# A decode step's last weight matrix: 128 of its rows moved to sixteen partitions by a transfer of their own

## The chip, the core and the metric

The kernel runs on one core of a Trainium2 chip. The metric is the device time of one execution in microseconds (us). TensorE (PE in the profile, its weight loads PEld) multiplies matrices, VectorE (DVE), ScalarE (ACT) and GpSimd (POOL) work on vectors, and SyncE (SP) issues nearly all transfers between the chip's memory (HBM) and the on-chip memory (SBUF). A core has 16 DMA engines; a transfer is shared out over several of them, and is done when the last of these is done. Matmul results go to the accumulators (PSUM).

## The reference

One decode step for a batch of B = 4 rows of width D = 576. Two branches read the same normalised input and are added to it:

```python
xn  = layernorm(x)
# A: attention over a window of 2048 keys, 16 kv heads of 128, 2 query heads each
q   = xn @ wq
p   = softmax(q . k_cache[:, :, -2048:] * 128**-0.5)
a   = (p . v_cache[:, :, -2048:]) @ wo
# B: a token mixer and an MLP, F = 4608
h   = gelu(layernorm(xn) @ w1)
x1  = xn + shifted(h) @ w2            # sequence length 1
b   = x1 + gelu(layernorm(x1) @ w3) @ w4
out = x + a + b
```

Nearly all the work is reading: the keys and the values are 33.5 MB each, wq and wo 4.7 MB each, w3 and w4 5.3 MB each. All of it is bf16.

## The kernel before

The kernel is one list of operations for each engine. `add` and `add_dma` put an operation on an engine's list with the signals that it waits for and a number, `key`; each list is then sorted by `key`, and an engine runs its list in that order. An operation with several waits starts after the last of them, and everything behind it on its engine waits too.

**Loads.** SP issues in this order: wq, w2, w1, w3, then the key blocks (one per kv head, 2 MB each, all 128 partitions, 16 KB a partition) into a ring of four slots (`kring`), the value blocks into another ring of four (`vring`), wo into the key ring after the keys, and last w4 into the value ring. A block's load waits until the block four before it has been used (`T...` for keys, `PV...` for values). Every one of these loads is issued at line 176, inside `add_dma`.

**w4.** `w4_src` (line 245) gives each partition p the RT = 36 consecutive rows 36p to 36p + 35 of w4, so that column t of the tile holds the rows 36p + t. The loads come in five pieces of rows per partition, `W4P = ((0, 14), (14, 28), (28, 33), (33, 35), (35, 36))`.

**Stages of TensorE.** The projections of q and of the mixer come first. Then `pe_h2` (line 527) multiplies the normalised x1 with w3 in five steps r (four of 128 rows, one for the rest), each into four groups of 32 columns of the array (j = 0..3, 1152 outputs each) and three accumulators (`CH2`). `gelu2` (line 537, three activations) applies gelu, and a transpose by VectorE (line 540) makes of it `h2T_sb`, the left operands of the w4 product. `zeroS` (line 340) waits for `gelu2` and opens the key stage: transposes of key blocks (line 351), their copies to SBUF (lines 358 and 359) and the scores (line 367). `SC15` is the last score product. After the softmax the value stage follows, a hardware loop over the 16 blocks (`PV`, line 448), each scaled by VectorE (line 456).

**The end.** After the value loop TensorE runs, in this order: `turn` (line 474), which waits for the last scaling; `AO` (line 463, 64 matmuls), the product with wo, which waits for `ORT`, the copy of `turn`'s result by VectorE (line 477); `MO0` (line 463, 28 matmuls), rows 0 to 13 of each partition of w4; `fold` (line 543, 8 matmuls with an ACT copy at line 553 before it), which adds up four partial accumulators; `MO1` to `MO4` (line 543, 88 matmuls), the other pieces of w4, each waiting for its piece. `AO` and `MO0` use four column groups of the array in turn (`acc_mm`, 288 columns wide), `MO1` to `MO4` two (`fin_mm`, 144 wide). Two copies to `out_sb` (lines 570 and 571) and two stores end the kernel.

```python
def acc_mm(e, h, lhsT, rhs, start=False, stop=False, k0=0):
    return e.matmul(ACC[h], lhsT=lhsT, rhs=rhs, start=start, stop=stop, tile_position=(k0, 32 * h))
...
add("pe", pe_turn, waits=[("c", ("on", m), NIT + 1) for m in range(4)] + ["sel32"], sig="turn", key=KV + 19.9)
...
add("pe", pe_AO, waits=["ORT", ev_wo], sig="AO", key=KV + 20)
```

Of the kernel before, what the change touches and what calls it, by code (L numbers as in the profile page):

```python
# [6 lines left out]
BF16 = mybir.dt.bfloat16  # L7
ACTF = mybir.ActivationFunctionType
# [11 lines left out]
WO_AFTER = 3  # L20
V0_AFTER = 8
FOLD = 14
W4P = ((0, 14), (14, 28), (28, 33), (33, 35), (35, 36))


class Op:
# [12 lines left out]
def bass_parallel_sum__sliding_block_cached__mixer_s_mlp__decode_kernel(  # L39
    nc, A_x, A_k_cache, A_v_cache, A_wq, A_wo, B_x, B_w1, B_w2, B_w3, B_w4, out  # L40
):
    B, Sq, D = A_x.shape
    _, Hkv, Sk, Dh = A_k_cache.shape
    Hq = A_wq.shape[1] // Dh
    F = B_w3.shape[1]
    W = min(4096, max(256, Sk // 4))
    assert (B, D, Hkv, Dh, Hq, W, Hq // Hkv, F) == (4, 576, 16, 128, 32, 2048, 2, 4608)
    G = Hkv
# [4 lines left out]
    EPS = 1e-5  # L53
    HALF = D // 2
    FH = F // 2
    RT = F // 128
    N2 = F // 4
    CH2 = [(0, 12), (12, 24), (24, 32)]
    x2 = A_x.rearrange("b s d -> (b s) d")
    o2 = out.rearrange("b s d -> (b s) d")  # L60
# [1 line left out]
    with ExitStack() as ctx:  # L62
        def sb(name, shape, dt):
            return ctx.enter_context(nc.sbuf_tensor(name, shape, dt))
# [7 lines left out]
        regB_t = sb("regB", [128, max(NKT * 1024, W3E)], BF16)  # L72
# [4 lines left out]
        w3main = regB_t[:, 0:4 * F].rearrange("p (r n) -> p r n", r=4)  # L77
        w3rag = regB_t[:, 4 * F:W3E]
# [23 lines left out]
        x1nT = sb("x1nT", [128, 6, 32], BF16)  # L102
        hs_inT = sb("hs_inT", [128, 10, B], BF16)
        h2T_sb = sb("h2T_sb", [128, RT, 32], BF16)
        Qpad_t = sb("Qpad", [128, 130 * G], BF16)
        Qpad = Qpad_t[:, 0:128 * G].rearrange("p (g b c) -> p g b c", g=G, b=B)
        Qs = sb("Qs", [128, 4, B, 32], BF16)
# [14 lines left out]
        PTb = sb("PTb", [128, NT * 32], BF16)  # L122
# [13 lines left out]
        ps = ctx.enter_context(nc.psum_tensor("ps", [128, 8, 512], FP32))[:]  # L136
# [13 lines left out]
        H2ps = [ps[:, k, 0:RT * (z - a)] for k, (a, z) in enumerate(CH2)]  # L150
        h_sb = PTs[0:B].rearrange("p t r -> p (t r)")[:, 0:D]
        xsrc = PTs[0:B].rearrange("p t r -> p (t r)")[:, 640:1920].rearrange("b (s p) -> b s p", s=10)
        h2a = PTb[:, 0:N2].rearrange("p (c i) -> p c i", i=32)

        S = {}
        for nm in ("pe", "dve", "act", "pool"):
# [8 lines left out]
        def add(engine, emit, waits=(), sig=None, key=0.0, loop=None):  # L165
            seqc[0] += 1
            prog[engine].append(Op(emit, waits, sig, key, seqc[0], loop))

        def add_dma(pairs, skey, waits=(), key=0.0, engine="sp"):
            if skey not in S:  # L170
                S[skey] = sem("s_" + "_".join(str(k) for k in (skey if isinstance(skey, tuple) else (skey,))))
            dma_count[skey] = dma_count.get(skey, 0) + 16 * len(pairs)

            def emit(e):
                for o_, i_ in pairs:
                    e.dma_start(o_, i_).then_inc(S[skey], 16)  # L176
            add(engine, emit, waits, None, key)
            return ("dma", skey, dma_count[skey])
# [4 lines left out]
        KS = float(NHB + 4)  # L183
        KV = KS + 4.0
# [3 lines left out]
        P = lambda *a, **k: add("pool", *a, **k)  # L188
# [3 lines left out]
                                    pattern=[[-1, 128]], channel_multiplier=1), waits=["ib1"], sig="ident_bf", key=-98)  # L192
        P(lambda e: e.memset(ragsrc[:], 0.0), sig="rag_zero", key=-97)
        P(lambda e: e.memset(xsrc, 0.0), sig="xs_zero", key=-96.8)
        P(lambda e: e.memset(xnT[:], 0.0), sig="xnT_zero", key=-96.6)
        P(lambda e: e.memset(Qpad_t[:], 0.0), sig="qpad_zero", key=-96)
        P(lambda e: e.memset(x1nT[:], 0.0), sig="x1nT_zero", key=-95.9)
# [2 lines left out]
        def first_counts(e):  # L200
# [37 lines left out]
        for g in range(G):  # L238
            kk = KS + g if g else V0_AFTER + 0.5
            w = [f"PV{g - NVS}"] if g >= NVS else (["hT"] if g < WQ_SLOTS else [])  # L240
            ev_v.append(add_dma(kv_pairs(vring_t, g % NVS, A_v_cache, g), ("v", g % NVS), w, kk))
            if g == WO_AFTER:
                ev_wo = add_dma([(kring_t[:, 0:32 * D], A_wo.rearrange("(p r) n -> p (r n)", r=32))],
                                "wo", [wo_wait], kk + 0.1)
        w4_src = B_w4.rearrange("(p r) n -> p r n", r=RT)
        w4_sb = vring_t[:, 0:RT * D].rearrange("p (t n) -> p t n", n=D)
        for n, (t0, t1_) in enumerate(W4P):
            lst = (t1_ * D - 1) // UE
# [124 lines left out]
        for n in range(NHB):  # L373
            p = n % 32
            w = [("L", ("k", p // 8), 16)] if p % 8 == 0 else []
            w.append(("L", ("eb", (p - NTB) % 32), 1))
            add("pe", pe_T(n), waits=w, sig=f"T{n}", key=n // 32 + 0.01 * p, loop=("k", n // 32))
            eng, f = evac(n)
            add(eng, f, waits=[f"T{n}"] + ([f"SC{n // 8 - 2}"] if n >= 8 else []), sig=("eb", p), key=n + 0.2)
        for g in range(-1, G):  # L380
            s_ = g % 4
            if g < G - 1:
                add("pe", pe_SC(g), waits=[("L", ("eb", 8 * s_ + 6), 1), ("L", ("eb", 8 * s_ + 7), 1), ("L", ("qs", s_), 1)], sig=f"SC{g}",
                    key=(g + 1) // 4 + 0.01 * (8 * ((g + 1) % 4) + 1) + 0.005, loop=("k", (g + 1) // 4))
            else:
                add("pe", pe_SC(g), waits=[("c", ("eb", 30), NIT + 1), ("c", ("eb", 31), NIT + 1), ("c", ("qs", 3), NIT + 1)],
                    sig=f"SC{g}", key=NIT + 0.5)
        for g in range(G):
            P(lambda e, g=g: e.tensor_copy(out=Qs[:, g % 4], in_=Qpad[:, g]), waits=(["qT"] if g == 0 else []) + ([f"SC{g - 4}"] if g >= 3 else []),  # L389
              sig=("qs", g % 4), key=8 * g)  # L390
# [4 lines left out]
            waits=["rmax"], sig="negb", key=KS + 0.05)  # L395
        for q in range(4):
# [65 lines left out]
        def acc_mm(e, h, lhsT, rhs, start=False, stop=False, k0=0):  # L462
            return e.matmul(ACC[h], lhsT=lhsT, rhs=rhs, start=start, stop=stop, tile_position=(k0, 32 * h))  # L463
# [53 lines left out]
        def pe_h2(r):  # L517
            def f(e):
                ins = None
                for k, (a, z) in enumerate(CH2):  # L520
                    for j in range(4):
                        c0, n = N2 * j + RT * a, RT * (z - a)
                        if r < 4:
                            w, x_ = w3main[:, r, c0:c0 + n], x1nT[:, r, :]
                        else:
                            w, x_ = w3rag[:, c0 % FH:c0 % FH + n], x1nT[:, 4 + j // 2, :]
                        ins = e.matmul(H2ps[k][32 * j:32 * j + 32, :], lhsT=x_, rhs=w, start=(r == 0), stop=(r == 4), tile_position=(0, 32 * j))  # L527
                return ins
            return f
        KW = -10  # L530
# [3 lines left out]
        def gelu2(e):  # L534
            ins = None
            for k, (a, z) in enumerate(CH2):
                ins = e.activation(out=h2a[:, :, a:z], in_=H2ps[k].rearrange("p (i c) -> p c i", c=RT), func=ACTF.Gelu_apprx_tanh)  # L537
            return ins
        add("act", gelu2, waits=["h2_4"], sig="gelu2", key=KW + 0.1)
        add("dve", lambda e: e.transpose(h2T_sb[:].rearrange("p c i -> p (c i)"), PTb[:, 0:N2]), waits=["gelu2"], sig="h2T", key=KW + 0.2)  # L540

        def fin_mm(e, h, z, lhsT, rhs, start=False, stop=False):
            return e.matmul(FIN[h][z], lhsT=lhsT, rhs=rhs, start=start, stop=stop, tile_position=(0, 32 * h))  # L543
# [1 line left out]
        def pe_fold(e):  # L545
            ins = None
            for z in range(2):
                for h in range(2):
                    ins = fin_mm(e, h, z, sel_h[0:96 + B, h, :], fold_sb[0:96 + B, OC * z:OC * (z + 1)], start=True)
            return ins  # L550
        n_fold = [z for _, z in W4P].index(FOLD)
        assert FOLD % 2 == 0
        add("act", lambda e: e.activation(out=fold_sb[0:96 + B, :], in_=ps[0:96 + B, 0, 0:HALF], func=ACTF.Copy),  # L553
# [104 lines left out]
```

## Time and profile before

| | |
|---|---|
| median of 3 runs | 214.77 us (214.70 to 214.79) |
| the profiled execution: time | 214.71 us |
| the profiled execution: span from the first to the last instruction | 213.5 us |
| granted TensorE clock, mean over the span | 0.784 |
| read from HBM | 88.49 MB, 415 GB/s over the span |
| busy: PE, DVE, ACT, POOL | 65%, 41%, 28%, 6% |

The profile is of one execution. Its page gives the busy time of each engine, the DMA engines' share in 40 slices of the span, the DMA queues with the packets that they moved, and the chain of waits that ended last. Other views answer from the trace: the groups of instructions by line, the timeline of a stretch (start, duration, engine, line, operation, count, and in brackets the idle time before and what ended it), and tables of windows (busy time of each engine with its count of instructions, granted clock, mean busy share of the 16 DMA engines, GB/s). A time stands in us from the start of the span unless ns is written.

### The profile page before, as it was taken

The page shows a single profiled execution, that of the slowest core. Times are in us where ns is not written, and L with a number is a line of the kernel's source. Part 1 is how long each engine was busy: PE and PEld are TensorE (multiplying, and loading weights), DVE is VectorE, ACT ScalarE, POOL GpSimd, SP SyncE. Part 2 cuts the span into 40 slices and gives each one's busy share as a digit, 9 for nine tenths or more (in the row PEclk, how much of TensorE's full clock was granted, in tenths as well). Part 3 has the DMA queues.
Part 4 walks back from the last instruction along what each step waited for, and adds up shares of the span by engine and source line. Part 5 has one row for each costly group of instructions (what it writes and reads, how often), then busy time and mean ns, then how long its engine had stood idle before and what let it go on. Part 6 is the DMA issues. An engine that isn't in the chain of part 4 may idle for free.

```text
span 213.5 us, 5829 instructions
## 1 busy us (share of the span) xinstructions
PE 137.9 (65%) x2692; PEld 108.8 (51%) x2692; DVE 87.3 (41%) x162; ACT 59.5 (28%) x72; POOL 12.0 (6%) x39
## 2 busy tenths in 40 slices
PE   0088147999999992999999818923343443333596
PEld 0036023777888881788888702923343443333444
DVE  6715203666666662266666649721111112100000
ACT  2001302665555563156665655000000000000000
POOL 8501000000000000000000000000000000000000
PEclk9999859999999998599999995555555555555569
DMA  6999989999999999999999999999999999999993
GB/s 246 430 401 498 438 363 433 433 416 421 433 430 427 421 433 433 427 424 431 430 418 439 427 436 442 424 418 430 414 430 436 424 427 430 439 411 435 426 407 129
DMA packets 6513, 88.63 MB, mean 415 GB/s; under 512 B 732, under 2 KB 872, under 8 KB 1640
## 3 DMA queue, kind: packets, MB, share of 16 engines
q1 hardware_dynamic: 6488, 88.50, 97.8%
q8 instruction: 7, 0.11, 0.2%
q10 hardware_dynamic: 16, 0.01, 0.0%
q14 instruction: 2, 0.02, 0.0%
HBM read 88.49 MB, written 0.00 MB: 415 GB/s over the span
## 4 chain that ended last, share of the span: by engine, by line
DMA 52%; PE 39%; DVE 4%; issue 2%; SPq 1%; ACT 1%
PE ps L351 23%; DMA vring<-in_A_v_cache_dram 23%; DMA regB<-in_B_w_dram 12%; DMA kring<-in_A_k_cache_dram 9%; DMA vring<-in_B_w_dram 8%; PE ps L367 7%; PE ps L448 4%; PE ps L527 2%; PE ps L543 1%; DVE PTb L401 1%; SPq L176 1%; DVE rmax L393 1%; DVE regB L359 1%; ACT PTb L537 1%; DVE PTs L409 1%
## 5 line engine op out<-in xcount | busy, mean ns | idle before, releaser
L359 DVE COPY regB<-ps 128x1024 bf16<-128x1024 bf16 x80 | 52.4, 688 | 34.0 <-PE ps L351 32.1
L351 PEld LDWEIGHTS ps<-perm_k,kring 128*128 128x128 bf16 x1024 | 58.9, 99 | 12.4 <-issue 7.8
L351 PE MATMUL ps<-perm_k,kring 128*128 128x128 bf16 x1024 | 62.4, 222 | 4.2 <-DMA kring<-in_A_k_cache_dram 4.1
L358 ACT ACTIVATE regB<-ps 128x1024 bf16<-128x1024 bf16 x48 | 47.8, 1023 | 40.6 <-PE ps L351 40.5
L448 PE MATMUL ps<-PTg,vring 128*128 128x8 bf16 x1024 | 29.5, 168 | 38.1 <-DMA vring<-in_A_v_cache_dram 36.5
L448 PEld LDWEIGHTS ps<-PTg,vring 128*128 128x128 bf16 x1024 | 28.4, 104 | 39.2 <-DMA vring<-in_A_v_cache_dram 27.5
L456 DVE TENSOR_TENSOR PTb<-ps,PTb 128x32 bf16<-128x32 f32 x16 | 3.1, 192 | 55.3 <-PE ps L448 55.2
L367 PE MATMUL ps<-regB,Qs 128*32 128x512 bf16 x272 | 18.6, 395 | 4.4 <-issue 3.1
L553 ACT ACTIVATE P_sb<-ps 100x288 f32<-100x288 f32 x1 | 0.4, 411 | 75.2 <-PE ps L463 75.2
L367 PEld LDWEIGHTS ps<-regB,Qs 128*32 128x32 bf16 x272 | 6.6, 97 | 10.6 <-issue 6.0
L412 DVE TENSOR_TENSOR PTg<-PTs,bmask 128x512 bf16<-128x512 bf16 x16 | 10.7, 682 | 0.0
L389 POOL COPY Qs<-Qpad 128x128 bf16<-128x128 bf16 x16 | 4.6, 296 | 92.0 <-PE ps L367 82.5
L527 PE MATMUL ps<-regB,x1nT 128*32 128x432 bf16 (+1 forms) x60 | 3.9, 431 | 7.1 <-DMA regB<-in_B_w_dram 7.1
L527 PEld LDWEIGHTS ps<-regB,x1nT 128*32 128x32 bf16 x60 | 1.9, 123 | 8.8 <-DMA regB<-in_B_w_dram 7.2
L540 DVE STREAM_TRANSPOSE h2T_sb<-PTb 128x1152 bf16<-128x1152 bf16 x1 | 1.4, 1379 | 12.0 <-ACT PTb L537 12.0
L402 PE MATMUL ps<-PTb,perm_p 128*128 128x512 bf16 x4 | 2.4, 608 | 4.3 <-DVE PTb L401 4.1
L293 PE MATMUL ps<-ident_bf,xn_bf 4*128 4x4 bf16 x4 | 0.3, 166 | 7.5 <-DVE ragsrc L277 7.5
L570 DVE CAST out_sb<-ps 36x144 bf16<-36x144 f32 x1 | 0.3, 300 | 9.9 <-PE ps L543 9.9
L463 PE MATMUL ps<-kring,ORT 128*4 128x288 bf16 x64 | 4.0, 443 | 0.4 <-DVE ORT L477 0.4
L315 PE MATMUL ps<-vring,xnT 128*32 128x512 bf16 x40 | 4.2, 597 | 0.0
L293 PEld LDWEIGHTS ps<-ident_bf,xn_bf 4*128 4x128 bf16 x4 | 0.2, 110 | 7.4 <-POOL ones_f L213 7.4
L537 ACT ACTIVATE PTb<-ps 128x432 bf16<-128x432 f32 (+1 forms) x3 | 1.3, 491 | 8.6 <-PE ps L527 8.6
(99 smaller groups left out, 76.9 us busy)
## 6 DMA issues: line engine op xcount, KB each, us to landing
kring<-in_A_k_cache_dram SPq DMA_DIRECT2D x16, 2048.0 KB, 16.7
vring<-in_A_v_cache_dram SPq DMA_DIRECT2D x16, 2048.0 KB, 17.6
regB<-in_B_w_dram SPq DMA_DIRECT2D x1, 4608.0 KB, 26.1
kring<-in_A_wo_dram SPq DMA_DIRECT2D x1, 4608.0 KB, 22.7
vring<-in_A_wq_dram SPq DMA_DIRECT2D x2, 2048.0 KB, 9.5
vring<-in_B_w_dram SPq DMA_DIRECT2D x2, 2016.0 KB, 17.4
vring<-in_B_w_dram SPq DMA_DIRECT2D x2, 648.0 KB, 13.7
vring<-in_B_w_dram SPq DMA_DIRECT2D x1, 720.0 KB, 14.3
```

The source lines that it names most:

```text
L315: ins = e.matmul(Qps[32 * j:32 * j + 32, k, :], lhsT=x_, rhs=w, start=(r == 0), stop=(r == 4), tile_position=(0, 32 * j))
L351: ins = e.transpose(tb[n % NTB][:, t, :], kring[:, g % NKS, 8 * k + t, :], perm_k[:])
L358: return "act", lambda e: e.activation(out=ktbuf[:, n % NKT], in_=src, func=ACTF.Copy)
L359: return "dve", lambda e: e.tensor_copy(out=ktbuf[:, n % NKT], in_=src)
L367: ins = e.matmul(Sps[32 * b:32 * b + 32, c4, :].rearrange("p (t i) -> p t i", t=16), lhsT=Qs[:, g % 4, b, :], rhs=kttile[:, t0:t0 + 16, b, :],
L389: P(lambda e, g=g: e.tensor_copy(out=Qs[:, g % 4], in_=Qpad[:, g]), waits=(["qT"] if g == 0 else []) + ([f"SC{g - 4}"] if g >= 3 else []), ...
L412: add("dve", lambda e, g=g: e.tensor_tensor(out=PTg[:, g % NPG], in0=PTs[:, :, 2 * g:2 * g + 2].unsqueeze(2).to_broadcast([128, NT, B, 2]) ...
L448: ins = e.matmul(OTps(g), lhsT=vring[:, g % NVS, t, :], rhs=PTg[:, g % NPG, t].rearrange("p b e -> p (b e)"), start=(t == 0), stop=(t == N ...
L456: add("dve", lambda e, g=g: e.tensor_tensor(out=OTx[:, :, 2 * g:2 * g + 2, :], in0=OTps(g).rearrange("p (b e) -> p b e", b=B).unsqueeze(3) ...
L463: return e.matmul(ACC[h], lhsT=lhsT, rhs=rhs, start=start, stop=stop, tile_position=(k0, 32 * h))
L527: ins = e.matmul(H2ps[k][32 * j:32 * j + 32, :], lhsT=x_, rhs=w, start=(r == 0), stop=(r == 4), tile_position=(0, 32 * j))
L537: ins = e.activation(out=h2a[:, :, a:z], in_=H2ps[k].rearrange("p (i c) -> p c i", c=RT), func=ACTF.Gelu_apprx_tanh)
```

## The change

The last 128 rows of w4 (rows 4480 to 4607) are taken out of the large layout. The other 4480 rows stand 35 a partition, and the pieces are `((0, 14), (14, 28), (28, 32), (32, 34), (34, 35))`. The 128 rows go to partitions 0 to 15 of `regB` (the tile that held w3 and then the transposed keys), eight rows each, by one transfer `w4x` whose source has the outermost dimension 4 (`e`), then 4 (`c`), then eight rows in one run. It is issued by SP behind the load of value block 5 and waits for `SC15`.

So `pe_h2` covers 4480 columns of w3 with 1120 a group, and the last 128 columns go to a fourth accumulator (bank 3, group 0); where a group's columns cross the middle of w3's ragged part the matmul is cut in two. `gelu2` has a fourth activation (32x128, its result ordered by the new layout), VectorE a second transpose (32x256, `h2Tx`), and GpSimd zeroes `h2ax` at the start. The product with the 128 rows is 16 matmuls of 16 rows and 288 columns, `MX0` (eight of them, between the value loop and `turn`) and `MX1` (eight, between `turn` and `AO`), into the accumulators of the column groups 0 and 1.

```diff
-W4P = ((0, 14), (14, 28), (28, 33), (33, 35), (35, 36))
+W4P = ((0, 14), (14, 28), (28, 32), (32, 34), (34, 35))
+XROWS = 128
+XE, XC, XT = 4, 4, 8
+X_AFTER = 5
...
-    RT = F // 128
-    N2 = F // 4
+    RT = (F - XROWS) // 128
+    FM = RT * 128
+    N2 = FM // 4
...
+        h2Tx = sb("h2Tx", [32, XT, 32], BF16)
+        w4x = regB_t[0:XE * XC, 0:XT * D].rearrange("p (t n) -> p t n", n=D)
...
-        w4_src = B_w4.rearrange("(p r) n -> p r n", r=RT)
+        x_src = B_w4[FM:F, :].rearrange("(c e t) n -> e c (t n)", c=XC, e=XE)
+        ev_w4x = add_dma([(regB_t[0:XE * XC, 0:XT * D], x_src)], "w4x", [f"SC{G - 1}"], KS + X_AFTER + 0.2)
+        w4_src = B_w4[0:FM, :].rearrange("(p r) n -> p r n", r=RT)
...
+                    todo = [(k, j, N2 * j + RT * a, RT * (z - a)) for j in range(4)]
+                    if k == 2:
+                        todo.append((3, 0, FM, XROWS))
+                    for bk, j, c0, n in todo:
+                        cuts = [c0, c0 + n] if r < 4 or not c0 < FH < c0 + n else [c0, FH, c0 + n]
...
+            return e.activation(out=h2ax[:, :, 0:XE * XC].rearrange("p t (e c) -> p t e c", c=XC),
+                                in_=H2x.rearrange("p (c e t) -> p t e c", c=XC, e=XE), func=ACTF.Gelu_apprx_tanh)
+        add("act", gelu2, waits=["h2_4", "h2ax_zero"], sig="gelu2", key=KW + 0.1)
+        add("dve", lambda e: (e.transpose(h2Tx[:].rearrange("p t i -> p (t i)"), PTb[0:32, N2:N2 + 32 * XT]),
+                              e.transpose(h2T_sb[:].rearrange("p c i -> p (c i)"), PTb[:, 0:N2]))[1], waits=["gelu2"], sig="h2T", key=KW + 0.2)
...
+        for n in range(2):
+            def f(e, n=n):
+                ins = None
+                for t in range(XT // 2 * n, XT // 2 * (n + 1)):
+                    for h in range(2):
+                        ins = acc_mm(e, h, h2Tx[0:XE * XC, t, 0:B], w4x[:, t, HALF * h:HALF * (h + 1)])
+                return ins
+            add("pe", f, waits=[ev_w4x, "h2T"], sig=f"MX{n}", key=KV + 19.8 + 0.15 * n)
```

More of the change, by code (lines that the diff above doesn't have):

```diff
@@ L55, in bass_parallel_sum__sliding_block_cached__mixer_s_mlp__decode_kernel @@
     FH = F // 2
-    RT = F // 128
-    N2 = F // 4
+    RT = (F - XROWS) // 128
+    FM = RT * 128
+    N2 = FM // 4
+    assert XE * XC * XT == XROWS and RT == W4P[-1][1]
     CH2 = [(0, 12), (12, 24), (24, 32)]
@@ L153, in bass_parallel_sum__sliding_block_cached__mixer_s_mlp__decode_kernel @@
         h2a = PTb[:, 0:N2].rearrange("p (c i) -> p c i", i=32)
+        H2x = ps[0:32, 3, 0:XROWS]
+        h2ax = PTb[0:32, N2:N2 + 32 * XT].rearrange("p (t i) -> p t i", i=32)
         S = {}
@@ L194, in bass_parallel_sum__sliding_block_cached__mixer_s_mlp__decode_kernel @@
         P(lambda e: e.memset(xsrc, 0.0), sig="xs_zero", key=-96.8)
+        P(lambda e: e.memset(h2ax, 0.0), sig="h2ax_zero", key=-86)
         P(lambda e: e.memset(xnT[:], 0.0), sig="xnT_zero", key=-96.6)
@@ L520, in f @@
                 for k, (a, z) in enumerate(CH2):
[L521 to L527, printed above, removed]
+                    todo = [(k, j, N2 * j + RT * a, RT * (z - a)) for j in range(4)]
[3 more added lines that the diff above has]
+                        cuts = [c0, c0 + n] if r < 4 or not c0 < FH < c0 + n else [c0, FH, c0 + n]
+                        for c, d in zip(cuts, cuts[1:]):
+                            if r < 4:
+                                w, x_ = w3main[:, r, c:d], x1nT[:, r, :]
+                            else:
+                                w, x_ = w3rag[:, c % FH:c % FH + d - c], x1nT[:, 4 + c // FH, :]
+                            ins = e.matmul(ps[32 * j:32 * j + 32, bk, c - c0:d - c0], lhsT=x_, rhs=w, start=(r == 0), stop=(r == 4 and d == c0 + n),
+                                           tile_position=(0, 32 * j))
                 return ins
@@ L537, in gelu2 @@
                 ins = e.activation(out=h2a[:, :, a:z], in_=H2ps[k].rearrange("p (i c) -> p c i", c=RT), func=ACTF.Gelu_apprx_tanh)
-            return ins
-        add("act", gelu2, waits=["h2_4"], sig="gelu2", key=KW + 0.1)
-        add("dve", lambda e: e.transpose(h2T_sb[:].rearrange("p c i -> p (c i)"), PTb[:, 0:N2]), waits=["gelu2"], sig="h2T", key=KW + 0.2)
+            return e.activation(out=h2ax[:, :, 0:XE * XC].rearrange("p t (e c) -> p t e c", c=XC),
[3 more added lines that the diff above has]
+                              e.transpose(h2T_sb[:].rearrange("p c i -> p (c i)"), PTb[:, 0:N2]))[1], waits=["gelu2"], sig="h2T", key=KW + 0.2)
         def fin_mm(e, h, z, lhsT, rhs, start=False, stop=False):
```

## The prediction

> **What bounds the kernel now.** The page comes first: its slices, its queues and the shares of the chain.
>
> ```profile
> span 213.5 us, 5829 instructions
> POOL 8501000000000000000000000000000000000000
> DMA  6999989999999999999999999999999999999993
> q1 hardware_dynamic: 6488, 88.50, 97.8%
> q8 instruction: 7, 0.11, 0.2%
> q10 hardware_dynamic: 16, 0.01, 0.0%
> DMA 52%; PE 39%; DVE 4%; issue 2%; SPq 1%; ACT 1%
> ```
>
> The 16 DMA engines are busy 97.8% of the span, from the second slice to the last but one. So the kernel is as long as its reading, plus what follows the last byte. The change reads the same bytes. What it can move is which engine ends last, and the work behind that. The chain of waits, its last part:
>
> ```profile
> 151.76 17.64 DMA vring<-in_A_v_cache_dram
> ...
> 171.34 17.65 DMA vring<-in_A_v_cache_dram
> ...
> 190.93 17.48 DMA vring<-in_B_w_dram
> 208.41 0.04 issue
> 208.46 3.13 PE ps L543 x88
> 211.61 0.30 DVE out_sb L570
> ```
>
> The two value blocks landed at 169.40 and 188.99: four blocks of 2048 KB in 19.6 us, 4.9 us each, 428 GB/s, 26.75 GB/s for each engine. At 208.41 the second piece of w4 lands, then 88 matmuls run. The timeline of the end, and windows over it (TensorE, its loads, DVE, ACT, POOL, granted clock, DMA share, GB/s):
>
> ```profile
> 198.81 1.87 PE L448 MATMUL ps<-PTg,vring 128*128 128x8 bf16 x64 [3.02 <-DMA vring<-in_A_v_cache_dram]
> ...
> 201.16 0.27 PE L474 MATMUL ps<-sel,PTb 128*128 128x32 bf16 x4 [0.48 <-DVE PTb L456]
> ...
> 201.81 4.01 PE L463 MATMUL ps<-kring,ORT 128*4 128x288 bf16 x64 [0.38 <-DVE ORT L477]
> 205.61 1.45 PE L463 MATMUL ps<-vring,h2T_sb 128*4 128x288 bf16 x28
> ...
> 207.58 0.66 PE L543 MATMUL ps<-P_sb,sel_h 100*4 100x144 f32 x8 [0.52 <-ACT P_sb L553]
> 208.46 2.66 PEld L543 LDWEIGHTS ps<-vring,h2T_sb 128*4 128x4 bf16 x84 [0.53 <-DMA vring<-in_B_w_dram]
> 208.46 3.11 PE L543 MATMUL ps<-vring,h2T_sb 128*4 128x144 bf16 x88 [0.21 <-DMA vring<-in_B_w_dram]
> 211.28 0.09 PEld L543 LDWEIGHTS ps<-vring,h2T_sb 128*4 128x4 bf16 x4 [0.16 <-DMA vring<-in_B_w_dram]
> ```
> ```profile
> 206.00:208.00 2.00, 1.48 (x36) 0.74 (x24) 0.00 (x0) 0.41 (x1) 0.00 (x0) 0.88 0.95 393
> 208.40:209.00 0.60, 0.54 (x18) 0.54 (x20) 0.00 (x0) 0.00 (x0) 0.00 (x0) 1.00 0.97 374
> 209.00:209.40 0.40, 0.40 (x20) 0.40 (x15) 0.00 (x0) 0.00 (x0) 0.00 (x0) 1.00 0.69 274
> 209.80:210.20 0.40, 0.40 (x20) 0.38 (x13) 0.00 (x0) 0.00 (x0) 0.00 (x0) 1.00 0.46 179
> 210.40:210.90 0.50, 0.50 (x20) 0.40 (x14) 0.00 (x0) 0.00 (x0) 0.00 (x0) 1.00 0.29 101
> 210.95:211.20 0.25, 0.25 (x10) 0.17 (x8) 0.00 (x0) 0.00 (x0) 0.00 (x0) 1.00 0.00 0
> ```
>
> Two things are to be seen. First, TensorE ran MO1 to MO4 nearly without a pause, and only the last four loads waited (0.16 us, at 211.28, for the last piece): reading and multiplying end almost together. Second, the DMA engines do not end together. All run at 209.0; around 210.0 the share is 0.46, 7.4 engines of 16; after 210.95 none. The 0.69 puts the end of the early ones at about 209.15, the 0.29 that of the late ones at about 210.7: seven are late by some 1.55 us. The page counts seven instruction packets (q8) beside the data. I read it so: each of these fell on another engine and put it behind for good, because its queue never runs empty. Every piece waits for the late seven.
>
> **The change, part by part.** *The late engines.* A row of 128 x 1152 bytes is 9,216 bytes an engine, 0.34 us at 26.75 GB/s. The late seven lose it behind MO1's piece, so that piece still lands at 208.41 and the later ones up to 0.34 us earlier. TensorE has 84 matmuls for 88: their 84 loads took 2.66 us, and from the last load group (211.28 and 0.09) to the copy at 211.61 are 0.24 us. From 208.46 that is 211.36, against 211.61: 0.25 us less. Without any pause inside the 84 it would be a little more: 0.33 at most, the 0.16 of the wait and the 0.09 of the four loads, with some hundredths from the other pieces' waits. I take 0.25.
>
> *The four engines.* The moved rows are 147,456 bytes. The load of x and one store (q10: 16 packets for two transfers of four partitions, four of data and four of completion each) show that a transfer of four partitions runs on four engines. I take it that an outermost dimension of 4 gives four engines here too: 36,864 bytes each, 1.38 us. That is less than the 1.55 us by which an early engine is ahead. So four early ones still end some 0.2 us before the late ones, and this part costs nothing. If one of the four is late, MO1's piece lands 1.38 us later. Both ends stay in the range of cases below.
>
> [...]
>
> *MX0 and MX1*, 16 matmuls on TensorE's way to MO1, which leave room in two waits (0.48 us before `turn`, 0.38 before `AO`):
>
> ```profile
> L496 PE MATMUL ps<-vring,hs_inT x18: 284/286/286, 17.2 to 19.3; 128*4 128x288 bf16 x18
> ```
>
> The lower price is `AO`'s, the same width over four column groups: 4.01 us by 64, 63 ns, 1.0 us for 16. The upper price comes from line 496, the same width without groups at the full clock: 17 steps in 2.1 us, 124 ns; at half the clock and with two groups side by side again 124 ns, 2.0 us. MX uses two groups, so I take 2.0. Less the 0.86 us of waits, `AO` starts 1.1 us later (0.1 at the lower price). The window 206 to 208 has a clock of 0.88, so the clock doubles at about 206.5. Of the work pushed past that point half is won back: 0.55 us at the fold. MO1 has 0.21 us of waiting to spare, so it starts up to 0.34 us late. At the lower price, or where the clock doubles as much earlier as TensorE's unbroken run begins earlier (about 200.7 instead of 201.81), it starts on time. Between 0 and 0.34 I take 0.05 to 0.1, near the on-time end: `AO` ran 4.7 us before the clock came, and MX lengthens just this run.
>
> [...]
>
> *The w3 product, gelu and transposes*, and one small fill by POOL, which is busy in the first four slices only:
>
> ```profile
> 29.79 3.88 PE L527 MATMUL ps<-regB,x1nT 128*32 128x432 bf16 x60 [7.07 <-DMA regB<-in_B_w_dram]
> ...
> 33.73 1.25 ACT L537 ACTIVATE PTb<-ps 128x432 bf16<-128x432 f32 x3 [8.60 <-PE ps L527]
> 35.01 1.38 DVE L540 STREAM_TRANSPOSE h2T_sb<-PTb 128x1152 bf16<-128x1152 bf16 x1 [11.96 <-ACT PTb L537]
> ```
> ```profile
> kring<-in_A_k_cache_dram SPq DMA_DIRECT2D x16, 2048.0 KB, 16.7
> kring<-in_A_wo_dram SPq DMA_DIRECT2D x1, 4608.0 KB, 22.7
> ```
> ```profile
> 117.37 0.34 SPq L176 DMA_DIRECT2D kring<-in_A_wo_dram  x1
> 134.95 0.54 SPq L176 DMA_DIRECT2D vring<-in_A_v_cache_dram  x1
> ```
>
> Each step streams 1120 + 128 columns for 1152: 8% of 3.88, 0.3 us. The fourth activation costs up to 1.25 by 3, 0.4 us, and the 256 columns more of transpose 0.3 us. `zeroS` waits for gelu, so the key stage starts some 0.7 us later (0.3 to 1.0). This I cost at nothing: a key block lands 16.7 us after its issue and takes 4.9 us, so over 11 us of reading are queued ahead of it. The thinnest cover is at 134.95, where the next value block is issued while wo has until 140.1 to run (117.37 + 22.7), 5.1 us for the late engines and 3.5 for the early ones. Only a delay over 3.5 us would let engines run dry.
>
> *SP* has one more issue, of about 0.5 us, among value blocks that are issued 4.9 us apart; its wait for SC15 is over by then.
>
> *Sum*: -0.25 + 0 + (0.05 to 0.1) + 0 = about -0.2 us. The profiled execution (214.71, span 213.5) becomes 214.5; the median stood 0.06 above it, so 214.55.
>
> **The rivals.** *A late engine among the four (slower).* Place: MO1's landing. Price: 1.38 us, so MO1 at 209.8, end 1.38 - 0.25 = 1.1 later: 215.9. It decides as soon as one of the four is one of the seven. Were they drawn at random, none late would have 9x8x7x6 by 16x15x14x13, 7%. I put the chance of a late one far lower, at 12%: joining each packet's end to the next one's start in the trace by hand, which no view prints and which is ambiguous in places, the instruction packets fell on engines that started after those that loaded x. That is a judgement, not a row.
>
> *A half-late engine among them.* Engines that end between the two groups are in the 0.69. One 0.8 us behind the early ones would carry MO1's piece 0.8 + 1.38 - 1.55 = 0.6 late, end about 0.35 later: 215.1.
>
> *TensorE's path becomes the bound.* MX at 2.0 us with nothing won back by the clock, so `AO` 1.1 late and MO1 0.9 late: 0.6 slower, 215.4. It decides once MO1 is held up by over 0.25 us.
>
> *One more instruction packet on an engine that is already late*: 1.55 more, 216.1. The program grows by some dozens of its 5829 instructions, so this is unlikely.
>
> *The late engines come off better.* If the changed program has its instruction packets at other moments, MO1 may land earlier, but TensorE is not free before 208.24: 0.21 more, 214.3.
>
> **How the numbers follow.** 0.2% is 0.43 us, about what a measurement of this kernel can tell from no change. Forecast 44% (its own range 214.4 to 214.75), late engines better off 18%, a late one among the four 12%, half-late 12%, TensorE's path 10%, one packet more 4%. The forecast and two thirds of the half-late case lie within 0.2%: 52%. Faster by more: 18%. Slower by more: 12 + 10 + 4 + 4 = 30%. The range 214.2 to 215.4 leaves out the late one and the packet, 16%.
>
> **What would show it.** Right: the last load group at 211.28 no longer waits for the last piece, MO1 starts within 0.1 us of 208.46, the copy at about 211.4; the DMA share near 210 stays at or under seven engines; `AO` starts at about 202.9 while the fold ends no more than 0.3 us later. Wrong: MO1 starts near 209.8 after a wait for a DMA (a late engine among the four), or follows the fold without a wait (TensorE's path); more than seven instruction packets; a DMA share that sags before 200.

## The result and the profile after

The changed kernel took 215.68 us (median of 21 runs, 215.04 to 216.90) against 214.79 us for the kernel before (21 runs, 214.60 to 214.88). The ratio is 1.0043, with a 95% interval of 1.0034 to 1.0053: slower by 0.43%, outside the predicted range of 214.2 to 215.4. The runs of the changed kernel lie 1.9 us apart, those of before 0.3. The six at 216.04 and above are the six whose mean granted clock was 0.778; the other fifteen had 0.784 or 0.785. In the kernel before, means from 0.776 to 0.792 left no mark on the time.

The profiled execution took 215.47 us (before: 214.71), so it shows 0.76 us of the change and stands 0.21 us below the median. Its page:

```profile
span 214.2 us, 5868 instructions
q8 instruction: 8, 0.13, 0.3%
q14 instruction: 2, 0.02, 0.0%
DMA 46%; PE 43%; DVE 4%; issue 3%; ACT 1%; SPq 1%
```

In the shares of the chain DMA falls from 52% to 46% and PE rises from 39% to 43%. The chain itself says where (start, duration, what it ran through):

```profile
162.31 17.64 DMA vring<-in_A_v_cache_dram
...
180.00 1.89 PE ps L460 x64
...
181.90 17.62 DMA vring<-in_A_v_cache_dram
...
199.57 1.87 PE ps L460 x64
201.44 1.05 PE ps L475 x8
...
202.71 5.86 PE ps L475 x97
...
209.05 3.30 PE ps L562 x92
```

Before, the last transfer in the chain was a piece of w4, landing at 208.41. Now it is the last value block, and from 199.57 on TensorE alone sets the end. The timeline of the same stretch, in the form shown in the prediction (`PV` is line 460 now, `acc_mm` 475, `turn` 486, `fin_mm` 562):

```profile
199.57 1.87 PE L460 MATMUL ps<-PTg,vring 128*128 128x8 bf16 x64 [3.02 <-DMA vring<-in_A_v_cache_dram]
...
201.37 1.12 PE L475 MATMUL ps<-regB,h2Tx 16*4 16x288 bf16 x8
...
202.42 0.29 PE L486 MATMUL ps<-sel,PTb 128*128 128x32 bf16 x4
...
202.64 1.12 PE L475 MATMUL ps<-regB,h2Tx 16*4 16x288 bf16 x8
...
203.69 3.99 PE L475 MATMUL ps<-kring,ORT 128*4 128x288 bf16 x64
...
207.49 1.05 PE L475 MATMUL ps<-vring,h2T_sb 128*4 128x288 bf16 x28
...
209.05 0.66 PE L562 MATMUL ps<-P_sb,sel_h 100*4 100x144 f32 x8 [0.52 <-ACT P_sb L580]
...
209.54 2.80 PE L562 MATMUL ps<-vring,h2T_sb 128*4 128x144 bf16 x84
...
212.38 0.30 DVE L597 CAST out_sb<-ps 36x144 bf16<-36x144 f32 x1 [9.34 <-PE ps L562]
```

Read against the rows of before, start by start:

| | before | after | later by |
|---|---|---|---|
| last value block on TensorE | 198.81 | 199.57 | 0.76 |
| `turn` | 201.16 | 202.42 | 1.26 |
| `AO` | 201.81 | 203.69 | 1.88 |
| `fold` | 207.58 | 209.05 | 1.47 |
| `MO1` | 208.46 | 209.54 | 1.08 |
| copy to `out_sb` | 211.61 | 212.38 | 0.77 |

There are three separate things in it. The value block is late before TensorE has run any of the new matmuls at the end: a loss on the side of the transfers. `AO` loses another 1.12 us to `MX0` and `MX1`, and `MO1` now follows `fold` without waiting for a DMA. The last 0.31 us are won back behind `MO1`, where 84 matmuls run without a stall. Windows over the end (columns as in the prediction):

```profile
206.00:208.00 2.00, 2.00 (x49) 1.23 (x40) 0.00 (x0) 0.00 (x0) 0.00 (x0) 0.62 0.95 387
207.00:207.50 0.50, 0.50 (x15) 0.29 (x11) 0.00 (x0) 0.00 (x0) 0.00 (x0) 0.50 1.07 447
207.50:208.00 0.50, 0.50 (x21) 0.38 (x16) 0.00 (x0) 0.00 (x0) 0.00 (x0) 0.98 0.88 328
209.80:210.20 0.40, 0.40 (x20) 0.40 (x16) 0.00 (x0) 0.00 (x0) 0.00 (x0) 1.00 0.63 231
210.40:210.90 0.50, 0.50 (x23) 0.50 (x18) 0.00 (x0) 0.00 (x0) 0.00 (x0) 1.00 0.11 39
210.95:211.20 0.25, 0.25 (x16) 0.25 (x11) 0.00 (x0) 0.00 (x0) 0.00 (x0) 1.00 0.07 23
```

The clock doubled at about 207.5, where it had done so at about 206.5 before (0.53 from 206.0 to 206.5, 1.00 from 206.5 to 207.0). Near 210.0 the DMA share is 0.63 for 0.46: ten engines are still at work, where the prediction named at most seven as the sign that the four moved ones had room. Near 210.65 it is 0.11 for 0.29: the late seven do lose their row. After 210.95 it is 0.07 for 0.00: about one engine is at work longer than any was before.

### The profile page after: what moved, and what is told of

The parts are those of the page before. It is cut to its first block, busy times and chain, and to the rows that moved or that the text cites. A ratio compares the mean times of both kernels' runs of the same rounds, so it can differ in the third digit from the quotient of the medians.

```text
span 214.2 us, 5868 instructions
## 1 busy us (share of the span) xinstructions
PE 137.7 (64%) x2708; PEld 110.0 (51%) x2710; DVE 87.4 (41%) x163; ACT 59.4 (28%) x73; POOL 12.2 (6%) x40
## 4 chain that ended last, share of the span: by engine, by line
DMA 46%; PE 43%; DVE 4%; issue 3%; ACT 1%; SPq 1%
DMA vring<-in_A_v_cache_dram 25%; PE ps L363 23%; DMA regB<-in_B_w_dram 12%; DMA kring<-in_A_k_cache_dram 9%; PE ps L379 7%; PE ps L460 6%; PE ps L475 3%; PE ps L543 2%; PE ps L562 2%; DVE PTb L413 1%; DVE rmax L405 1%; SPq L185 1%; DVE regB L371 1%; ACT PTb L554 1%; DVE PTs L421 1%
## 5 line engine op out<-in xcount | busy, mean ns | idle before, releaser
L363 PEld LDWEIGHTS ps<-perm_k,kring 128*128 128x128 bf16 x1024 | 58.2, 98 | 11.0 <-issue 6.9
L363 PE MATMUL ps<-perm_k,kring 128*128 128x128 bf16 x1024 | 61.4, 221 | 3.6 <-DMA kring<-in_A_k_cache_dram 3.6
L543 PE MATMUL ps<-regB,x1nT 128*32 128x420 bf16 (+2 forms) x66 | 4.6, 450 | 6.8 <-DMA regB<-in_B_w_dram 6.8
L543 PEld LDWEIGHTS ps<-regB,x1nT 128*32 128x32 bf16 x66 | 3.1, 135 | 8.1 <-DMA regB<-in_B_w_dram 6.9
L414 PE MATMUL ps<-PTb,perm_p 128*128 128x512 bf16 x3 | 1.8, 608 | 4.9 <-DVE PTb L413 4.8
L554 ACT ACTIVATE PTb<-ps 128x420 bf16<-128x420 f32 (+1 forms) x3 | 1.2, 482 | 9.0 <-PE ps L543 9.0
```

The costliest lines, as they stand in the source:

```text
L363: ins = e.transpose(tb[n % NTB][:, t, :], kring[:, g % NKS, 8 * k + t, :], perm_k[:])
L543: ins = e.matmul(ps[32 * j:32 * j + 32, bk, c - c0:d - c0], lhsT=x_, rhs=w, start=(r == 0), stop=(r == 4 and d == c0 + n), tile_position=( ...
```

## The experiments

Theory D: of the four engines that carry the 128 rows, at least one had too little time to spare, so every later transfer lands later. Theory P: the 16 matmuls lengthen TensorE's path, and how much of that is paid depends on when the clock doubles. Theory S, a guess of the author's, came up with the first results: a transfer loses time for all when its engines write partitions that other engines write at the same time. No view here names the engine that writes a partition, so the runs can show what a destination costs and not this cause. All ratios are to runs of the kernel before on the same chip. Every kernel is the changed kernel with the edit shown, unless it says that it is the kernel before.

### The product with the 128 rows left out

```diff
+        add("sp", lambda e: None, [ev_w4x], None, 10001)
...
-            add("pe", f, waits=[ev_w4x, "h2T"], sig=f"MX{n}", key=KV + 19.8 + 0.15 * n)
```

> The changed kernel without the 16 matmuls MX0 and MX1: the product with the 128 rows is left out, their transfer on four engines stays. D+P: the last value block stays at about 199.5 us and MO1 waits for its piece until about 209.2, the time 0.3 to 0.6 us above before. D alone: unchanged against the changed kernel, 0.9 above before. P alone: MO1 at 208.4, 0.25 below before.

215.11 us (214.95 to 215.40, 10 runs), ratio 1.0013 (1.0004 to 1.0023). The timeline, TensorE's matmuls and, for `MO1`, its weight loads:

```profile
199.64 1.87 PE L461 MATMUL ps<-PTg,vring 128*128 128x8 bf16 x64 [3.03 <-DMA vring<-in_A_v_cache_dram]
...
202.65 4.01 PE L476 MATMUL ps<-kring,ORT 128*4 128x288 bf16 x64 [0.38 <-DVE ORT L490]
...
209.31 2.59 PEld L563 LDWEIGHTS ps<-vring,h2T_sb 128*4 128x4 bf16 x84 [0.23 <-DMA vring<-in_B_w_dram]
209.31 2.79 PE L563 MATMUL ps<-vring,h2T_sb 128*4 128x144 bf16 x84
```

The loss parts in two: 0.57 us (215.68 less 215.11) goes with `MX0` and `MX1`, and so does nearly all of the spread; 0.28 us over the kernel before stays. The last value block is as late as with them, and `MO1`'s weight loads wait for a DMA, so that part lies with the transfers. (The time lies just under the 0.3 to 0.6 us that D and P together expected.)

### `MX0` and `MX1` over four column groups

```diff
-                    ins = acc_mm(e, 2 * (r % 2) + h, ORT[:, r:128:32], wo_sb[:, r, HALF * h:HALF * (h + 1)], start=(r == 1))
+                    ins = acc_mm(e, 2 * (r % 2) + h, ORT[:, r:128:32], wo_sb[:, r, HALF * h:HALF * (h + 1)])
...
-                        ins = acc_mm(e, h, h2Tx[0:XE * XC, t, 0:B], w4x[:, t, HALF * h:HALF * (h + 1)])
+                        ins = acc_mm(e, 2 * (t % 2) + h, h2Tx[0:XE * XC, t, 0:B], w4x[:, t, HALF * h:HALF * (h + 1)], start=(t == 1))
```

> The changed kernel with MX0 and MX1 spread over four column groups instead of two (1.0 us of matmuls instead of 2.0), all else as it is. D+P: AO starts 0.1 to 0.3 us after its place without MX instead of 1.05, the time lies 0.35 to 0.5 us above before, between the kernel without MX (0.28 above) and the changed one (0.9 above), and the runs lie closer together than those of the changed kernel. D alone: no change against the changed kernel. P alone: 0.1 to 0.2 below before.

215.10 us (215.04 to 215.31, 11 runs), ratio 1.0017 (1.0008 to 1.0026). The timeline:

```profile
201.34 0.65 PE L475 MATMUL ps<-regB,h2Tx 16*4 16x288 bf16 x8
...
202.14 0.65 PE L475 MATMUL ps<-regB,h2Tx 16*4 16x288 bf16 x8
202.71 3.65 PE L475 MATMUL ps<-kring,ORT 128*4 128x288 bf16 x64
...
209.20 2.79 PE L562 MATMUL ps<-vring,h2T_sb 128*4 128x144 bf16 x84 [0.80 <-DMA vring<-in_B_w_dram]
```

Eight matmuls take 0.65 us over four groups and 1.12 over two. With that `MO1` waits for its piece again (0.80 us), the time is that of the kernel without the product, and the runs lie 0.3 us apart as before. So P holds as a term of 0.57 us at the median, and it is the two column groups that make it. What remains, D's part, is the same with and without the product: 0.30 us, a little under the 0.35 to 0.5 expected. No version that computes everything beats the kernel before; this one comes near it, 0.17% slower.

### Probes: how late is the last of the four engines?

Four loads of 2, 4, 8 and 16 rows were put into the queue behind the load of the last value block, each with a small ACT copy that waits for it. A load of 4 rows is taken to run on the same four engines as `w4x` (the expectations call them the first four; no view names them), and so ends when the last of these has come to it. In a first form the probes had no copies:

```diff
+        prb = {pk: sb(f"prb{pk}x", [pk, 64], BF16) for pk in (2, 4, 8, 16)}
...
+        for q, pk in enumerate((2, 4, 8, 16)):
+            ev_prb = add_dma([(prb[pk][:], B_w1[0:pk, 0:64])], ("prb", pk), (), KS + 15.5 + 0.01 * q)
+            add("sp", lambda e: None, [ev_prb], None, 10001)
```

> The kernel before with four tiny transfers (2, 4, 8 and 16 rows of 128 bytes) behind the load of value block 15, nothing reads them. Each lands when the last of its engines has worked off its queue. D: 16 rows land with the latest engines, some 1.8 us after the earliest; 4 rows 0.5 to 1.1 us after the earliest, 0.7 to 1.3 before the 16 rows. Rival (late engines among the first four): 4 rows land with the 16 rows. Rival (the first four all early): 2, 4 and perhaps 8 rows land 1.6 to 1.8 us before the 16 rows.

Put into the kernel before it took 214.85 us, but the view of the transfers gives a landing time for the 16 rows alone, so it decided nothing. With ACT copies in place of the last line:

```diff
+            add("act", lambda e, pk=pk: e.activation(out=prb[pk][:], in_=prb[pk][:], func=ACTF.Copy), [ev_prb], f"prb{pk}", KT - 5 + 0.01 * q)
```

> The kernel before with four tiny transfers of 2, 4, 8 and 16 rows behind the load of value block 15, each followed by a tiny copy on ScalarE that starts when its transfer has landed, so that the timeline shows when the last of 2, 4, 8 and 16 engines has worked off its queue. D (engines among the first four are half-late before the change): the copy for 4 rows starts 0.5 to 1.2 us after the earliest engine (about 197.0) and at least 0.5 us before the copy for 16 rows. Rival, a fully late engine among the four: the copies for 4 and 16 rows start together. Rival, none even half-late: the copy for 4 rows starts within 0.4 us of the earliest engine.

> The same four probes in the changed kernel. D: the first four engines are now the latest of all, so the copies for 4, 8 and 16 rows start within 0.6 us of each other, the one for 4 rows at about 199.7 to 200.0, some 1.4 us later than in the kernel before. Rival (the 128 rows cost these engines less or nothing): the copy for 4 rows starts where it did before.

The kernel before with the probes took 214.88 us, the changed one 215.07, one run each. ACT's timeline in the kernel before:

```profile
197.83 0.26 ACT L254 ACTIVATE prb2x<-prb2x 2x64 bf16<-2x64 bf16 x1 [66.54 <-DMA prb2x<-in_B_w_dram]
198.27 0.26 ACT L254 ACTIVATE prb4x<-prb4x 4x64 bf16<-4x64 bf16 x1 [0.19 <-DMA prb4x<-in_B_w_dram]
198.90 0.26 ACT L254 ACTIVATE prb8x<-prb8x 8x64 bf16<-8x64 bf16 x1 [0.37 <-DMA prb8x<-in_B_w_dram]
199.15 0.26 ACT L254 ACTIVATE prb16x<-prb16x 16x64 bf16<-16x64 bf16 x1
```

and in the changed kernel:

```profile
199.26 0.26 ACT L266 ACTIVATE prb2x<-prb2x 2x64 bf16<-2x64 bf16 x1 [67.22 <-DMA prb2x<-in_B_w_dram]
199.67 0.26 ACT L266 ACTIVATE prb4x<-prb4x 4x64 bf16<-4x64 bf16 x1 [0.15 <-DMA prb4x<-in_B_w_dram]
199.87 0.26 ACT L266 ACTIVATE prb8x<-prb8x 8x64 bf16<-8x64 bf16 x1
200.05 0.26 ACT L266 ACTIVATE prb16x<-prb16x 16x64 bf16<-16x64 bf16 x1
```

Before the change the last of the four reached its probe 0.63 us ahead of the last of eight (which made ACT wait) and at most 0.88 us ahead of the last of sixteen (there ACT came straight from the copy before). So the slowest of the four had about 0.6 to 0.9 us to spare, not 1.55. In the changed kernel the four are 1.40 us later (198.27 to 199.67), which is the predicted 1.38, and nothing has to be waited for behind them: they are now among the latest. 1.38 less 0.6 to 0.9 is 0.5 to 0.8 us, and the last value block is 0.76 us late.

The packed traces keep one thing that none of these views prints: the moment at which each engine of a transfer counts its share as landed. In the changed kernel four engines count `w4x`, at 149.30, 149.62, 150.05 and 150.58 us. How far the sixteen engines stand behind the first of them, in us, in the block just before it in the queues and in the block after it:

| | block counted from 147.91 | block counted from 152.89 |
|---|---|---|
| early | eight, 0 to 0.37 | six, 0 to 0.28 |
| in between | 0.75 and 1.30 | none |
| late | six, 1.63 to 1.92 | six, 1.54 to 1.83 |
| moved by the 128 rows | | 1.31, 1.62, 2.06 and 2.59 |

Each of the four counts of `w4x` comes some 1.38 us behind a moment of the left column: the first engine's, one near 0.3, and those at 0.75 and 1.30. So the four were two early engines and both of those in between, and none of the late. The slowest had 0.6 us to spare (1.92 less 1.30) and ends 0.76 us behind the last of the late ones (2.59 less 1.83). In the last value block of the kernel before, the two in between are at 0.58 and 0.95 and the last engine is at 1.80.

The same moments show where the two in between come from. The page has, beside q8, two smaller instruction packets on q14 (0.02 MB), in the kernel before and after alike. They ran at 44.3 and 99.8 us before and at 44.5 and 95.0 after, and in both kernels the first engine in between appears in the first block counted after the one packet, the second in the first block after the other. Each packet of q8 before 200 us is followed in the same way by one more late engine. The trace gives the order in time; it does not name the engines.

### Half the rows

```diff
-        ev_w4x = add_dma([(regB_t[0:XE * XC, 0:XT * D], x_src)], "w4x", [f"SC{G - 1}"], KS + X_AFTER + 0.2)
+        ev_w4x = add_dma([(regB_t[0:XE * XC, 0:XT // 2 * D], x_src[:, :, 0:XT // 2 * D])], "w4x", [f"SC{G - 1}"], KS + X_AFTER + 0.2)
```

`MX0` and `MX1` are left out as above, and 64 of the 128 rows are not read.

> As the changed kernel without MX0 and MX1, but only four of the eight rows of each partition are loaded (64 of the 128 rows are not read at all): 18,432 bytes, 0.69 us, on each of the first four engines instead of 1.38. D: the half-late engines now end about with the late ones, the last value block begins at 198.8 to 199.0 instead of 199.6, MO1 near 208.4 to 208.6, the time 0 to 0.3 us below before. If half-late engines don't matter: no change against the kernel without MX, 215.1.

214.55 us (median of 10 runs). Nine lie between 214.34 and 214.85; one took 217.31 with a mean clock of 0.779, was not profiled, and remains unexplained; it widens the interval of the ratio to 0.9975 to 1.0029 around 1.0002. The timeline of the profiled execution (214.34 us):

```profile
198.86 1.87 PE L461 MATMUL ps<-PTg,vring 128*128 128x8 bf16 x64 [3.02 <-DMA vring<-in_A_v_cache_dram]
...
208.51 2.79 PE L563 MATMUL ps<-vring,h2T_sb 128*4 128x144 bf16 x84 [0.29 <-DMA vring<-in_B_w_dram]
```

With 0.69 us for each of the four engines (half of 1.38) the last value block and `MO1` are 0.05 us later than before. So the delay begins between 0.69 and 1.38 us, as the probes have it, and D is confirmed by a dose. Against 214.82 us for the kernel before on this chip the median is 0.27 us lower, and in the profile the copy to `out_sb` starts at 211.34 for 211.61: the gain at the end of w4, alone. The interval of the ratio, with the one long run in it, does not separate this gain from no change.

### Sixteen engines for the 128 rows

```diff
-XE, XC, XT = 4, 4, 8
+XE, XC, XT = 16, 1, 8
```

`w4x`, with an outermost dimension of 4, was counted by four engines; that a dimension of 16 puts it on all sixteen is taken from that.

> The same 128 rows, the same products, but the transfer's source has an outermost dimension of 16, so that each of the 16 DMA engines carries 9,216 bytes of it. Theory D+P (two causes: engines among the first four were already part of the way behind and become the last; and MX0 and MX1 hold up TensorE's path to MO1): the last value block is back at about 198.8 us (199.57 in the changed kernel), AO still starts about 1.1 us after its place before, MO1 between 208.5 and 209.0, the time 0 to 0.4 us above before. D alone: 0.25 us below before. P alone: no better than the changed kernel, 0.9 us above before.

And the same without the product:

> Both causes taken away: the transfer on 16 engines, the 16 matmuls left out (the product with the 128 rows is not computed). D+P: MO1 at 208.4 us as before, four matmuls fewer behind it and the last piece earlier: 0.25 to 0.33 us below before. If the larger w3 product, the fourth activation and the second transpose cost anything at the end, it shows here as less than that.

Both expectations missed. With the product it took 216.68 us (216.39 to 217.34, 4 runs), ratio 1.0091 (1.0071 to 1.0112); without it 216.55 (216.15 to 217.09, 4 runs), ratio 1.0079 (1.0058 to 1.0099). Spread over all engines the same bytes cost 1.4 us more than on four (216.55 against 215.11). The window in which the 128 rows are transferred, first with the product, on four engines (the changed kernel) and on sixteen:

```profile
148.00:152.00 4.00, 1.87 (x64) 1.78 (x64) 0.23 (x2) 0.00 (x0) 0.00 (x0) 0.50 1.01 431
```
```profile
148.00:152.00 4.00, 1.12 (x42) 1.12 (x43) 0.00 (x0) 0.00 (x0) 0.00 (x0) 0.50 1.00 285
```

and without the product, again on four and on sixteen:

```profile
148.00:152.00 4.00, 1.87 (x64) 1.78 (x64) 0.17 (x2) 0.00 (x0) 0.00 (x0) 0.50 1.00 427
```
```profile
148.00:152.00 4.00, 0.61 (x23) 0.61 (x24) 0.08 (x1) 0.00 (x0) 0.00 (x0) 0.50 0.98 271
```

On sixteen the engines are as busy (share 1.00 and 0.98), but 285 and 271 GB/s arrive in place of 431 and 427.

### The destination moved: three kernels

Sixteen engines, each writing one partition out of eight (0, 8, ..., 120), without the product:

```diff
-XE, XC, XT = 4, 4, 8
+XE, XC, XT = 16, 1, 8
...
-        ev_w4x = add_dma([(regB_t[0:XE * XC, 0:XT * D], x_src)], "w4x", [f"SC{G - 1}"], KS + X_AFTER + 0.2)
+        ev_w4x = add_dma([(regB_t[0:128:8, 0:XT * D], x_src)], "w4x", [f"SC{G - 1}"], KS + X_AFTER + 0.2)
```

> As the run with the transfer on 16 engines and without MX0 and MX1 (the product with the 128 rows is not computed), but the 16 destination partitions are 0, 8, 16, ... 120 instead of 0 to 15. Theory S (several engines that write the same few neighbouring partitions slow each other and the engine whose blocks go there): most of the loss goes, 214.5 to 215.1 us. Theory N (a transfer of 9 KB runs on 16 engines is slow in itself): it stays near 216.5.

215.98 us (215.72 to 216.10, 4 runs), ratio 1.0050 (1.0033 to 1.0067): between the two expectations, and neither is met. Of the 1.44 us that sixteen engines lost against four, 0.57 go; the window from 148 to 152 shows 336 GB/s:

```profile
148.00:152.00 4.00, 1.31 (x49) 1.32 (x50) 0.00 (x0) 0.00 (x0) 0.00 (x0) 0.50 0.98 336
```

Sharper is a pair with four engines, again without the product, and only the partitions changed:

```diff
-        ev_w4x = add_dma([(regB_t[0:XE * XC, 0:XT * D], x_src)], "w4x", [f"SC{G - 1}"], KS + X_AFTER + 0.2)
+        ev_w4x = add_dma([(regB_t[64:64 + XE * XC, 0:XT * D], x_src)], "w4x", [f"SC{G - 1}"], KS + X_AFTER + 0.2)
```

> As the changed kernel without MX0 and MX1, same four engines and same bytes, but to the partitions 64 to 79 instead of 0 to 15. [...] N: unchanged, 215.1.

and the same line with 32 in place of 64, to see whether only the lowest partitions are cheap:

> Four engines as in the change, but the destination is partitions 32 to 47 in place of 0 to 15; MX0 and MX1 left out, so the product with the 128 rows is not computed. [...] If only the lowest partitions are cheap, or each engine has one block of four partitions, the loss is that of 64 to 79: 217.15 within 0.4, GB/s about 250.

Partitions 64 to 79: 217.15 us (216.97 to 217.21, 4 runs), ratio 1.0105 (1.0088 to 1.0122). Partitions 32 to 47: 215.08 (214.94 to 215.24, 10 runs), ratio 1.0011 (1.0001 to 1.0020), the same as partitions 0 to 15 (215.11). The window of the one and of the other:

```profile
148.00:152.00 4.00, 0.57 (x21) 0.57 (x22) 0.00 (x0) 0.00 (x0) 0.00 (x0) 0.50 1.03 249
```
```profile
148.00:152.00 4.00, 1.87 (x64) 1.79 (x64) 0.14 (x2) 0.00 (x0) 0.00 (x0) 0.50 1.01 431
```

And where `MO1` stands with partitions 32 to 47, in the timeline:

```profile
209.33 2.79 PE L563 MATMUL ps<-vring,h2T_sb 128*4 128x144 bf16 x84 [0.34 <-DMA vring<-in_B_w_dram]
```

Three times the same rows, bytes and number of partitions, from a source of the same shape: 0 to 15 and 32 to 47 cost nothing beyond D, 64 to 79 cost 2.0 us (217.15 against 215.11). So it is not only the lowest partitions that are cheap, and the destination alone has a price. Why it has one is not shown: S remains a guess. The loss is not one of four engines alone either: by the moments at which engines count their shares, every engine is late behind the transfer to 64 to 79, the earliest by 1.7 us (it counts the next block at 154.77, for 153.05 with partitions 0 to 15). How the loss spreads is open. Why one partition out of eight still loses 0.87 us (215.98 against 215.11) is not settled.

### Twice the rows

```diff
-W4P = ((0, 14), (14, 28), (28, 32), (32, 34), (34, 35))
-XROWS = 128
-XE, XC, XT = 4, 4, 8
+W4P = ((0, 14), (14, 28), (28, 31), (31, 33), (33, 34))
+XROWS = 256
+XE, XC, XT = 4, 8, 8
```

> 256 rows instead of 128 on the four engines (eight partitions each, 34 rows a partition for the rest); MX0 and MX1 stay 16 matmuls of the same width, over 32 rows. D: the first four engines come 1.4 us later still: value block 15 begins near 200.9, MO1 waits for its piece until about 210.6, the time 1.4 to 1.8 us above before and the runs close together, because TensorE is ready before the data. P: the matmuls are as many as in the changed kernel, so its time and spread stay, 0.9 above before.

219.49 us (218.95 to 220.07, 4 runs), ratio 1.0216 (1.0195 to 1.0236): far more than any expectation. The experiment changed two things at once: the rows are twice as many, and they go to 32 partitions, 0 to 31, in place of 16. The window from 148 to 152 has a loss of GB/s like those of sixteen engines (285 and 271) and of partitions 64 to 79 (249):

```profile
148.00:152.00 4.00, 1.30 (x49) 1.31 (x50) 0.00 (x0) 0.00 (x0) 0.00 (x0) 0.50 1.10 293
```

How much of it belongs to the bytes and how much to the partitions, no run separates. So it is no dose for D; the half dose is.

## Why the prediction was wrong, point by point

**"The late engines" (-0.25): right.** From `MO1` to the copy 3.15 us became 2.84, the last load group no longer waits, and the half-dose kernel, which has this part without the others, stands 0.27 us below the kernel before.

**"The four engines" (taken as 0): the first step that failed.** The price of 1.38 us was right (1.40 by the probes), and none of the late engines is among the four: by the counts of `w4x` they are two early ones and the two in between. What failed is "So four early ones still end some 0.2 us before the late ones". It took two groups, early and late, from a DMA share of 0.69 at 209.2 and 0.46 at 210.0, although the same rows hold engines between the two. The slowest of the four had 0.6 to 0.9 us to spare, not 1.55. This is the rival "A half-late engine among them", which had 0.8 us behind the early ones, `MO1`'s piece 0.6 us late and an end 0.35 us later. Measured: the last value block 0.76 us late, `MO1`'s piece 0.74 to 0.87 (208.46 before; 209.20 with four column groups, 209.33 with partitions 32 to 47, both after a wait for the DMA), and an end 0.23 to 0.30 us later. The prediction's row shows q8 alone; the two packets of q14, behind which the two engines in between appear, are on the same page, and the prediction does not count them. By the order of starts it had judged that the instruction packets fell on other engines than the four; that holds for q8 and not for q14.

**"MX0 and MX1" (0.05 to 0.1): the second step that failed.** It measured 0.57 us at the median. The upper price was right: `AO` starts 1.12 us after what the value block explains, for 1.1 predicted. The choice "Between 0 and 0.34 I take 0.05 to 0.1, near the on-time end" was not. It rested on the clock doubling as much earlier as TensorE's run starts earlier, which was the author's assumption; no run shows it, nor the 0.05 to 0.1 us taken from it. Counted as the prediction counts, from the end of the last value block, the run started at 201.37 in place of 201.81, and the clock doubled at about 207.5, 1.0 later in place of 0.4 earlier. That count is also wrong in itself: with `MX0` right behind the block TensorE has no pause from 199.57 on, so 7.9 us of unbroken run went by before the clock doubled. Two more profiles place the moment, that of the changed kernel with the probes and that of the four column groups:

```profile
206.50:207.00 0.50, 0.50 (x23) 0.38 (x17) 0.00 (x0) 0.00 (x0) 0.00 (x0) 0.95 0.99 415
```
```profile
205.00:206.00 1.00, 1.00 (x28) 0.59 (x20) 0.00 (x0) 0.00 (x0) 0.00 (x0) 0.58 0.99 419
```

So it came at about 206.5 and 205.8 there. From the start of `MX0` to the doubling it took 6.1 us in the changed kernel, 5.2 with the probes (from 201.30) and 4.5 with four column groups (from 201.34), against 4.7 from the start of `AO` before. The first two run the same matmuls from `MX0` on, and differ by 0.9 us. So the moment moves between profiles, and it does not come a fixed time after the start of the run. What sets it no run here shows. A term that depends on such a moment has a spread and no fixed price, and that is what the runs of the changed kernel show: 215.04 to 216.90, the highest six with the lowest mean clock. That a late doubling makes these six is argued from their means; none of them was profiled.

**The two together.** The rivals were weighed one by one, at 12% for half-late and 10% for TensorE's path. Both came true: 0.28 and 0.57 us, in sum 0.85, for 0.89 measured between the medians. Their sum, 215.1 plus 215.4 less the forecast of 214.55, is 215.95, which the range left out.

**The parts costed at nothing: right.** The half-dose kernel has the longer w3 product, the fourth activation, the second transpose and SP's extra issue, and its value block is 0.05 us late. The eighth instruction packet (q8) cost nothing that shows either: in the changed kernel it runs at 212.1 us, when the reading is over, and the kernel with four column groups has eight, that without the product seven, at 215.10 and 215.11 us.

## What to carry to other kernels

Before some engines are given more bytes than others, measure how much each of them has to spare, for instance by small loads of 2, 4, 8 and 16 rows late in the queue; the slowest of the chosen ones decides, not the group that it seems to belong to (here it had 0.6 to 0.9 us where 1.55 was read, and the last value block came 0.76 us late). A small transfer in the shadow of large ones should be tried at more than one destination: partitions 0 to 15 and 32 to 47 gave 215.11 and 215.08 us, 64 to 79 gave 217.15. And work that is put in front of a wait on TensorE should be costed at the clock that the windows show there (0.50 here) and spread over all four column groups (0.65 us for eight matmuls, against 1.12 over two).

## What was not expected of the hardware

Where a small transfer goes mattered no less here than how many engines carry it: the destination cost 2.0 us (217.15 against 215.11), sixteen engines for four 1.4 us (216.55 against 215.11). 147 KB written to partitions 64 to 79 left the whole core at 249 GB/s for about 4 us, where the same bytes to partitions 32 to 47 left it at 431, and the DMA share was 1.03 and 1.01: the busy share did not say how many bytes moved. An engine that fell behind stayed behind in these profiles: the two that appear in between after the packets of q14, at 44 and 100 us, are still there in the last value block at 197 us (0.58 and 0.95 us behind the first engine). Eight matmuls of 16 rows and 288 columns took 1.12 us over two column groups and 0.65 over four, both at half the clock (0.50 from 201 to 203).
